# Turning chunk 3's last-chunk score units by DMA in the first batch, a new turning order, and earlier own units of the last chunk in the last batch

## The chip, the cores and the metric

The kernel runs on one core of one Trainium2 chip. The metric is the device time of one execution in microseconds (us). A ratio is the mean time of one kernel's fast runs over the mean of the other's fast runs of the same rounds, so it is not quite the ratio of the medians quoted beside it; the interval is of 95%.

## The reference, cut to what matters

```python
# attention: B, S, D = 8, 3008, 256; z has 64 columns
scores = (1 / S) * np.matmul(z, z.transpose(0, 2, 1))   # symmetric in the two positions
attn = np.maximum(scores, 0.0) ** 2
x = u * np.matmul(attn, v)
# feed-forward on all 24064 rows, d_ff = 2048
h = x @ w_in
g = h * (1.0 / (1.0 + np.exp(-1.702 * h)))
out = g @ w_out
```

The scores are symmetric, so a block of keys against queries, once computed, can be turned (transposed) and used again with keys and queries exchanged.

## The kernel before

A batch's 3008 positions make six chunks of up to 512 (chunk 5 is the last, 448 wide) and 24 key tiles of 128. A score unit `(i, jp)` is chunk `i` as queries against the two key tiles `2*jp` and `2*jp + 1`: one pair of matmuls, a ReLU on ScalarE, a square on VectorE. `attend(b, i)` then runs chunk `i` through all key tiles. For key tiles of lower chunks it reads blocks turned by SyncE's transposing DMA (`TT`, buffers `tt`). A part of chunk 5's own unit 11 is turned out of its unit 10, into a block named `al`; in the last batch chunk 5 opens with it.

The last chunk is a special case. Where `turned(b, i)` holds, chunk `i`'s units 10 and 11 are computed with the last chunk as queries and chunk `i` as keys. They serve chunk 5 as they stand and chunk `i` after a turn. Where it doesn't hold, both forms are computed. In batch 0 it held for chunk 4 only.

```python
    def turned(b, i):
        return i < NCH - 1 and (b > 0 or i > 3)

    def square(b, i, jp, sc):
        ...
        if jp // 2 > i and (turned(b, i) or jp < NU - 2):
            if b and i == 0 and LATE:
                ...
            elif b == 0 and jp < NU - 2:
                squared.setdefault((i, jp // 2), []).append(lambda: turn_unit(b, i, jp, a))
                while ORDER0 and len(squared.get(ORDER0[0], ())) == 2:
                    for turn_it in squared.pop(ORDER0.pop(0)):
                        turn_it()
            else:
                turn_unit(b, i, jp, a)

    ORDER0 = [(0, 1), (0, 2), (1, 2), (0, 3), (1, 3), (0, 4), (2, 3), (1, 4), (2, 4), (3, 4)]

    def attend(b, i, both=False):
        ...
        elif b == 0 and i in (3, 4):      # own key tiles, chunk 4's, the lower ones, the last chunk's
            js = js[own:-CB + 1] + js[:own] + js[-CB + 1:]
```

`ORDER0` fixes the order in which batch 0's pairs of blocks are turned: a pair goes out when it is at the head of the list and both its units are squared. A last-chunk unit is turned at once, at its place in the program. SyncE issues all of them in program order. The scores are interleaved with the steps of `attend` by a schedule: in chunk `i` at step `n`, take so many units. In batches from 0 to 6 the feed-forward begins inside chunk 4, in the last batch inside chunk 5.

## Time and profile before

| | before |
|---|---|
| first three runs | 1187.97 us median, 1187.69 to 1188.5 |
| all six runs of the comparison | 1188.24 us median, 1187.31 to 1188.84 |
| PE busy in the profile | 1176.8 of 1186.5 us |
| PE's longest holes after its start | 1.84 us in chunk 3 of batch 0, 1.83 us at the opening of the last chunk of the last batch |

In the views PE is TensorE (PEld its weight loads), DVE VectorE, ACT ScalarE, POOL GpSimd, SP SyncE. In a timeline a line has the start, the length, the engine, the source line, the operation with its tiles (output from input) and shapes, and a count; brackets give the idle time before it and what ended it. A line of waits has the total, the number and the longest. The lines of these views are in the prediction.

### The profile page before, as it was taken

How to read it: one execution, taken by the hardware profiler on the slowest of the kernel's cores; microseconds unless marked ns; L12 is line 12 of the kernel's file. 1: busy time of each engine (PE TensorE's matmuls, PEld its weight loads, DVE VectorE, ACT ScalarE, POOL GpSimd, SP SyncE). 2: the span in 40 equal slices, each digit the busy share in tenths (PEclk: the TensorE clock that was granted, in tenths of full speed). 3: DMA queues.
4: the chain of work that ended last, by engine and by line, in shares of the span. 5: the costliest groups of instructions: out<-in, count | busy, mean ns of one | idle time of the engine just before them, and what ended most of it. 6: DMA issues, size and time to landing. Idle time of an engine off the chain costs nothing.

```text
span 1186.5 us, 27918 instructions
## 1 busy us (share of the span) xinstructions
PE 1176.8 (99%) x11526; PEld 699.6 (59%) x11526; DVE 837.7 (71%) x1441; ACT 819.3 (69%) x997; POOL 226.6 (19%) x319
## 2 busy tenths in 40 slices
PE   9999999999999999999999999999999999999998
PEld 3446764467644676447754478544784457844577
DVE  6688865877758776587775877658786487763776
ACT  7778864688646887478764787657866578672785
POOL 5243101231012310133101430014200241001000
PEclk9999999999999999999999999999999999999999
DMA  9998677866787677855789457895558875694012
GB/s 218 162 146 134 124 146 133 85 110 135 141 135 84 108 151 144 134 78 95 157 146 133 78 94 153 158 115 96 114 126 167 109 97 105 143 163 90 1 37 73
DMA packets 378880, 142.88 MB, mean 120 GB/s; under 512 B 320032, under 2 KB 372640, under 8 KB 378752
## 3 DMA queue, kind: packets, MB, share of 16 engines
q1 hardware_dynamic: 320464, 99.39, 46.3%
q0 software_dynamic: 56768, 40.39, 23.5%
q8 instruction: 90, 1.47, 0.5%
q10 hardware_dynamic: 1520, 1.31, 0.3%
q14 instruction: 38, 0.31, 0.1%
HBM read 60.29 MB, written 24.64 MB: 72 GB/s over the span
## 4 chain that ended last, share of the span: by engine, by line
PE 96%; ACT 1%; DMA 1%; issue 1%; DVE 1%; SPq 0%; DVEq 0%; ACTq 0%
PE o L358 39%; PE hg L399 27%; PE st L518 24%; PE sc L235 5%; ACT rl L256 1%; DMA tt<-a 1%; PE yp L493 1%; DMA al<-a 0%; PE w L99 0%; DVE a L270 0%; ACT ZT L143 0%; SPq L277 0%; DVE ut L202 0%; ACT gf L407 0%; DVE WT L446 0%
## 5 line engine op out<-in xcount | busy, mean ns | idle before, releaser
L407 ACT ACTIVATE gf<-hg 128x1024 f32<-128x1024 f32 (+1 forms) x384 | 385.5, 1004 | 143.7 <-PE hg L399 121.4
L256 ACT ACTIVATE rl<-sc 128x1024 f16<-128x1024 f32 (+1 forms) x301 | 287.7, 993 | 153.7 <-PE sc L235 108.4
L358 PEld LDWEIGHTS <-V 64*128 64x128 f16 (+1 forms) x4052 | 218.0, 95 | 257.9 <-issue 16.3
L399 PE MATMUL hg<-xt,W 128*128 128x512 f16 (+1 forms) x1408 | 354.6, 374 | 0.0
L411 DVE TENSOR_SCALAR gt<-gf 128x1024 f16<-128x1024 f32 (+1 forms) x320 | 222.9, 697 | 137.2 <-ACT gf L407 134.5
L358 PE MATMUL o<-a,V 64*128 64x512 f16 (+3 forms) x2240 | 296.1, 368 | 0.2 <-DVE a L270 0.2
L270 DVE TENSOR_TENSOR a<-rl 128x1024 f16<-128x1024 f16 (+1 forms) x266 | 178.5, 675 | 123.3 <-ACT rl L256 122.6
L195 POOL DMA_DIRECT2D uq<-in_u_dram x188 | 127.8, 687 | 692.0 <-PE sc L235 456.4
L358 PE MATMUL o<-tt,V 64*128 64x512 f16 (+1 forms) x1510 | 232.1, 377 | 1.8 <-DMA tt<-a 1.8
L399 PEld LDWEIGHTS <-W 128*128 128x128 f16 x1536 | 139.3, 98 | 119.2 <-issue 2.6
L518 PEld LDWEIGHTS <-gt 128*128 128x128 f16 x2944 | 177.1, 98 | 32.2
L518 PEld LDWEIGHTS <-s 128*128 128x128 f16 x2208 | 133.7, 98 | 25.6 <-issue 0.5
L235 PE MATMUL sc<-ZT 64*128 64x512 f16 (+3 forms) x688 | 114.6, 356 | 0.7 <-ACT ZT L143 0.4
L518 PE MATMUL st<-WT,gt 128*128 128x128 f16 x1472 | 97.8, 219 | 0.0
L518 PE MATMUL st<-WT,s 128*128 128x128 f16 x1472 | 96.6, 219 | 0.2 <-ACT uP L530 0.2
L518 PE MATMUL st<-W,gt 128*128 128x128 f16 x1472 | 96.6, 219 | 0.0
L536 DVE SCALAR_TENSOR_TENSOR y<-st,uP 128x256 f32<-128x256 f32 (+1 forms) x144 | 57.9, 409 | 28.3 <-ACT uP L530 19.9
L530 ACT ACTIVATE uP<-st 128x256 f32<-128x256 f32 (+1 forms) x144 | 53.0, 368 | 31.5 <-DVE y L536 16.2
L375 DVE TENSOR_TENSOR xt<-o,ut 128x512 f16<-128x512 f32 x80 | 51.4, 684 | 27.6 <-PE o L358 27.6
L409 ACT ACTIVATE gt<-gf 128x1024 f16<-128x1024 f32 (+1 forms) x64 | 65.9, 1030 | 2.1
L474 DVE TENSOR_TENSOR s<-s,gt 128x1024 f16<-128x1024 f16 (+1 forms) x96 | 64.4, 671 | 1.1
L472 DVE TENSOR_TENSOR s<-gt 128x1024 f16<-128x1024 f16 (+1 forms) x96 | 64.8, 675 | 0.0
(53 smaller groups left out, 600.2 us busy)
## 6 DMA issues: line engine op xcount, KB each, us to landing
out_dram<-y SPq DMA_DIRECT2D x40, 512.0 KB, 3.6
uq<-in_u_dram POOLq DMA_DIRECT2D x156, 128.0 KB, 3.7
V<-in_v_dram POOLq DMA_DIRECT2D x35, 256.0 KB, 6.4
tt<-a SPq DMA_TRANSPOSE x232, 3.9
uq<-in_u_dram POOLq DMA_DIRECT2D x32, 112.0 KB, 4.6
out_dram<-y SPq DMA_DIRECT2D x7, 384.0 KB, 3.1
vst<-in_v_dram SPq DMA_DIRECT2D x3, 512.0 KB, 5.9
zst<-in_z_dram POOLq DMA_DIRECT2D x7, 192.0 KB, 8.4
```

The lines of the kernel that those rows point to most:

```text
L195: eng.dma_start(uq[k * QW:(k + 1) * QW, :n // QW].rearrange("t q c k -> t q (c k)"), src[:, :, cs])
L235: pe.matmul(sc[:, r, :q1 - q0], zt[h, 2 * kp + r, :], zt[h].rearrange("d n p -> d (n p)")[:, q0:q1], start=True, stop=True,)
L256: act.activation(rl[:, :, :n], sc[:, :, :n], AF.Relu, scale=csc)
L270: dve.tensor_tensor(a[:, :, :n], rl[:, :, :n], rl[:, :, :n], ALU.mult)
L358: ins = pe.matmul(acc[c][:, :n], V16[b][h, j].rearrange("p (c k) -> p k c", k=NCC)[:, c], weights(b, i, j)[h], start=(k, m) == first[c], s ...
L399: pe.matmul(hg[:, e, :n], W1[:, c, ff * P:(ff + 1) * P], XT[b, i][:, c, :n], start=(c == 0), stop=(c == NCC - 1),)
L407: act.activation(gf[:, :, :n], hg[:, :, :n], AF.Gelu_apprx_sigmoid, scale=1.0 / FSC)
L409: act.activation(g, gf[:, :, :n], AF.Copy, scale=FSC)
L411: dve.tensor_scalar(g, gf[:, :, :n], FSC, None, ALU.mult)
L472: dve.tensor_tensor(s_, a21, a22, ALU.add)
L474: dve.tensor_tensor(s_, ST[b, k, "S1", h], a11, ALU.subtract)
L518: pe.matmul(bank[:, m, :], lhs()[:, f, m, :], right[:, ff, :], start=name in ("P1", "P2", "P5") and m == 0 and ff == 0, stop=ff == NFF // ...
```

## The change

It means to save two score units in batch 0, to end the wait in chunk 3 by turning the pair (2,3) sooner, and to end the wait of the last batch by computing chunk 5's own units sooner. The whole diff:

```diff
     def turned(b, i):
 
-        return i < NCH - 1 and (b > 0 or i > 3)
+        return i < NCH - 1 and (b > 0 or i > 2)
...
-    ORDER0 = [(0, 1), (0, 2), (1, 2), (0, 3), (1, 3), (0, 4), (2, 3), (1, 4), (2, 4), (3, 4)]
+    ORDER0 = [(0, 1), (0, 2), (1, 2), (0, 3), (1, 3), (2, 3), (0, 4), (1, 4), (2, 4), (3, 4)]
...
-    SCHED_LAST = SCHED | {3: {n: 1 for n in (14, 34)} | {NJ: 2}, 4: {NJ: 2}, 5: {}}
+    SCHED_LAST = SCHED | {3: {n: 1 for n in (14, 34)} | {NJ: 2}, 4: {2: 2}, 5: {}}
...
     SCHED0 = {
...
-        3: {n: 1 for n in (0, 4, 8, 12, 16, 19, 29, 33, 37, 41, 45)} | {NJ: 2},
+        3: {n: 1 for n in (0, 5, 10, 15, 30, 34, 38, 42, 45)} | {NJ: 2},
```

## The prediction

> **What bounds the kernel now.** I read the page first, then the waits of the tensor engine, then its timeline around each wait.
>
> ```profile
> span 1186.5 us, 27918 instructions
> PE 1176.8 (99%) x11526; PEld 699.6 (59%) x11526; DVE 837.7 (71%) x1441; ACT 819.3 (69%) x997; POOL 226.6 (19%) x319
> ...
> PE 96%; ACT 1%; DMA 1%; issue 1%; DVE 1%; SPq 0%; DVEq 0%; ACTq 0%
> ```
>
> PE is busy 99% of the span, and the chain that ended last runs through PE for 96% of it. So the time moves only by PE work removed and by holes in PE's stream that close or open. The view of PE's waits gives all the holes:
>
> ```profile
> PE o L358 <- DMA tt<-a: 1.8, 1, 1.8
> PE o L358 <- DMA al<-a: 1.8, 1, 1.8
> PE w L99 <- DVE nil L75: 1.2, 1, 1.2
> PE sc L235 <- ACT ZT L143: 0.4, 1, 0.4
> ```
>
> Two single waits of 1.8 us are all there is to win besides work, and the change aims at both. Timeline of PE in batch 0, chunk 3 (start, length, instruction, count, idle before):
>
> ```profile
> 52.92 1.03 PE L358 MATMUL o<-tt,V 64*128 64x512 f16 x8
> 53.78 0.35 PE L235 MATMUL sc<-ZT 64*128 64x448 f16 x2
> 55.98 0.82 PE L358 MATMUL o<-tt,V 64*128 64x512 f16 x6 [1.84 <-DMA tt<-a]
> ```
>
> A step is two matmuls, side by side on half the rows each. From the start of chunk 3, whose first score unit begins at 49.52, four groups of x8 run to 53.78, which is 16 steps: the hole stands ahead of step 16. By the order of the code (own four key tiles, the four of chunk 4, then 0 to 11) that step reads key tile 8, the first block turned from chunk 2: the pair (2,3) of the turning order. Timeline of PE in the last batch, where chunk 5 opens with key tile 23, taken from `al`:
>
> ```profile
> 1091.95 0.81 PE L358 MATMUL o<-tt,V 64*128 64x512 f16 x6
> 1094.60 0.37 PE L358 MATMUL o<-al,V 64*128 64x448 f16 x2 [1.83 <-DMA al<-a]
> ```
>
> The third view is the one that decides. All turns of blocks are issued by SyncE in program order. The view of the tile `tt` from 38 to 60 us:
>
> ```profile
> L298 SPq DMA_TRANSPOSE tt<-a x10: 1260/2173/4512, 35.8 to 59.3; - x10
> ...
> DMA to landing us min/median/max: 4.5/8.0/10.1
> ```
>
> An issue takes at least 1.26 us but here 2.17 us in the median, and 8.0 us to landing, against 3.9 us in the median of the whole kernel (the row of issues of the page). SyncE is full: from 35.77 to 65.31 it does nothing but turn blocks:
>
> ```profile
> 35.77 29.54 SPq L298 DMA_TRANSPOSE tt<-a  x11
> ```
>
> From the single issues in the trace, in order of issue, with landings (us): (1,3) 34.40 and 35.77, landed 42.01 and 45.84; (0,4) 38.90 and 42.81, landed 48.21 and 49.84; (2,3) 45.59 and 47.92, landed 50.85 and 55.94; (1,4) 49.52 and 51.11, landed 57.47 and 59.09; (2,4) 55.73 and 57.93, landed 61.65 and 62.42; (3,4) 59.29 and 61.34, landed 69.28 and 71.51; then the two last-chunk units of chunk 4, landed 72.33 and 73.28. The sources were ready long before: (2,3)'s second unit was squared by 37.31. The queue, not the data, sets these times.
>
> **What the Trainium skill says.** First, "TensorE: Matmul & The Clock Gate", section "Wait — 56ns, not 53.3ns?": a warm 512-column matmul follows its predecessor after 215.7 ns, a cold one after 426.7 ns. The trace agrees: the eight matmuls from 52.92 to 53.78, four pairs of row tiles, take 0.2155 us a step. Second, the same page, section "What's actually happening": after an idle window of about 3.4 us the array drops to half clock, and comes back after about 3.4 us of sustained work. In the trace the first seven matmuls take 3.04 us, 0.43 us each, which is the cold pace; the existing holes of 1.8 us are too short to show the drop. Third, "DMA: Bandwidth & Descriptors", section "Issuing engines are not separate DMA queues": transfers of all issuers share 16 engines and interleave. The trace agrees: turns land 0.9 us apart at 33.11, 33.98 and 34.88, with no load of another queue beside them, and none lands from 50.85 to 55.94 while the loads of `u` issued by GpSimd at 47.60 to 50.17 land. Fourth, its section "Latency and other measured facts" gives 261 GB/s for a transposing DMA; one turn is 128x1024 f16, 262 KB, so 1.0 us, close to the 0.9 us seen.
>
> **The change, part by part.**
>
> Part one, two units less. Chunk 5 of batch 0 no longer computes (5,6) and (5,7); chunk 3's units 10 and 11 are taken as 448-column scores of the last chunk, used as they stand in chunk 5 and turned for chunk 3. PE: a 448-column pair costs 0.19 us (a unit starts at 52.73, the next step at 52.92), twice makes 0.38 us; two units become 448 instead of 512 wide, 0.05 us. Together -0.43 us. ScalarE loses 2 x 0.92 us and VectorE about 2 x 0.63 us and gains 2 x 0.22 us: neither is the bound there, so nothing.
>
> Part two, (2,3) ahead of (0,4). In the queue (2,3) takes the places of (0,4), so it lands at about 48.2 and 49.8 instead of 50.85 and 55.94. PE wants it at 54.0. The hole of 1.84 us closes: -1.84 us.
>
> Part three is what I think is overlooked. Chunk 3 now needs two more turns, of its units 10 and 11, for its key tiles 20 to 22 (step 20 on) and 23. They are squared early (step 24 of chunk 2, by about 46 us), but turn in program order: moving (2,3) up lets (0,4) and (1,4), long complete, be flushed in the same breath, and (2,4) follows at step 3 of chunk 2. All eight stand ahead. So the two new turns get the places that (3,4) had before: issue 59.29 and 61.34. PE reaches step 20 at 49.47 + 20 x 0.2155 + four units before it (0.19 + 0.2155 + 0.2155 + 0.19 = 0.81) = 54.6.
>
> When do they land? Not at 69.28 and 71.51 as (3,4) did: those were slowed by the weight loads issued at 58.67 to 60.07, and they stand behind a GpSimd wait for PE's step 23 of this very chunk, so while PE is held they aren't issued. Free of them, the second new turn starts at 60.6 (59.29 + 1.26) to 61.3, and an unhindered issue takes 3.3 us to landing (the last batch: issued 1039.32, landed 1042.64). That gives 63.9 to 64.6; I take 64.1. PE needs both turns for any of its key tiles 20 to 23, since each fills half the columns. New hole: 64.1 - 54.6 = 9.5 us.
>
> Then the clock. A hole of 9.5 us holds a whole idle window, so PE should restart cold. An estimate from the page's 3.4 us at half clock: 1.7 us lost.
>
> The rest of the chunk: 27 steps x 0.2155 = 5.82 us and seven units of chunk 5 (six of 0.19 and one of 192 columns, 0.08), 1.22 us: 64.1 + 7.04 = 71.1 warm, 72.8 with the cold stretch. Before, it ended at 64.07 (55.98 + 31 steps, 6.68, + eight units, 1.41). So batch 0 ends 8.8 us later; the parts give -0.43 - 1.84 + 9.5 + 1.7 = +8.9, the same within the rounding. I use +8.8. Weight loads and the next batch's `z` shift with PE, as they hang on it, so their slack in chunk 4 stays about what it was, and a PE-bound remainder gives nothing back.
>
> Part four, last batch. The last chunk's own units go from step 24 to step 2 of chunk 4: 22 steps, 4.7 us earlier. SyncE is idle there from 1082.59 (waits until 1089.46 for these units). `al` then lands at 1094.46 - 4.7 = 1089.8, and PE wants it at 1092.77. The hole of 1.83 us closes: -1.83 us.
>
> Sum: 1187.97 + 8.8 - 1.8 = 1195.0 us, +0.6%.
>
> **Rivals.** (a) The change works as meant: the new turns come in time, and both holes close. Then 1187.97 - 0.43 - 1.84 - 1.83 = 1183.9 us. For it: the author surely meant it, and units 10 and 11 are squared 9 us before use. Against it: eight turns ahead of them in a queue that needs 2.2 us for each. (b) The hole opens but without a cold clock or with a brisker queue: landing near 62.5 and no half clock takes 1.6 + 1.7 us off the sum: 1191.7 us. For it: part of the queue's slowness from 59.5 to 61 coincides with an instruction fetch that a held PE may not make. (c) The turns are as slow as (3,4) was, landing at 71.5: a hole of 16.9 us in place of 9.5, 1202.4 us. Against it: its cause, the weight loads, waits for PE. (d) ScalarE or VectorE become the bound: in chunk 3 there are two units fewer over the same steps, so no.
>
> **Range and chances.** The landing of the second new turn is uncertain by about 1.5 us each way and the cold stretch by about 1 us; the repeats of the kernel before differ by 0.8 us. That makes 1191.8 to 1198. Rival (a), which I give 1 in 12, lies below it. Two per cent are 23.8 us either way: faster would need more holes than there are, slower more than rival (c). Faster 0.01, same 0.97, slower 0.02.
>
> **What would show it.** Right: in PE's waits the `al` line is gone, the `tt` line stands alone with about 9.5 us once, at about 54.6 us, ahead of matmuls that read the turned last-chunk block; after it several matmul steps at twice 0.2155 us; PE instructions down by 2 pairs of scores; chunk 4 begins about 72.8. Wrong: no hole near 54.6, or a landing of the twelfth turn counted from (1,3) before 60; a new hole in chunk 4 (weights late) would make it slower than said; a hole at the opening of the last chunk would undo part four.

## The result, and the profile after

| | median | range | runs |
|---|---|---|---|
| before | 1188.24 us | 1187.31 to 1188.84 | 6 |
| changed | 1196.60 us | 1193.77 to 1199.57 | 6 |

The ratio is 1.0072 (1.0054 to 1.0089): slower by 0.7%, inside the 2% that count as the same. The changed kernel also scatters more: its runs spread over 5.8 us, those of before over 1.5 us.

The page of the changed kernel:

```profile
span 1195.1 us, 27911 instructions
PE 1178.8 (99%) x11522; PEld 699.4 (59%) x11522; DVE 836.5 (70%) x1441; ACT 818.0 (68%) x995; POOL 227.7 (19%) x319
...
PEclk9989999999999999999999999999999999999999
```

PE has four matmuls less, which are the two units, and still is busy 2 us longer. The third digit of the clock row has fallen from 9 to 8, so something slowed PE's clock between 60 and 90 us. PE's waits:

```profile
PE o L358 <- DMA tt<-a: 10.2, 1, 10.2
PE w L99 <- DVE nil L75: 1.2, 1, 1.2
PE sc L235 <- ACT ZT L143: 0.3, 1, 0.3
```

The wait on `al` is gone. The wait on `tt` is still a single one, but of 10.2 us. The timeline of PE around it, in chunk 3 of batch 0:

```profile
53.88 0.35 PE L235 MATMUL sc<-ZT 64*128 64x448 f16 x2
54.07 1.24 PE L358 MATMUL o<-tt,V 64*128 64x512 f16 x10
65.54 1.89 PE L358 MATMUL o<-tt,V 64*128 64x512 f16 x8 [10.23 <-DMA tt<-a]
67.22 0.95 PE L235 MATMUL sc<-ZT 64*128 64x448 f16 x4
```

PE runs past step 16, where the old hole was, and stops at step 20, the first that reads the newly turned last-chunk block. Eight matmuls after it take 1.89 us; before, eight took 1.03 us. The table of stretches says why. A line has the start and the end, the length, the busy time (and instructions) of PE, PEld, DVE, ACT and POOL, the granted clock as a share of the full one, and DMA's share and GB/s:

```profile
54.10:65.50 11.40, 1.21 (x12) 0.36 (x8) 1.32 (x2) 0.92 (x1) 0.00 (x0) 0.67 1.19 164
65.50:68.20 2.70, 2.66 (x14) 1.02 (x16) 0.00 (x0) 0.36 (x1) 0.17 (x1) 0.50 1.00 189
68.20:74.40 6.20, 6.20 (x58) 2.67 (x55) 4.58 (x7) 5.55 (x8) 2.94 (x4) 1.00 1.07 151
```

The clock dropped to half inside the hole and came back only at 68.2, so 2.7 us of work ran at half speed.

The queue of turns, counted from (1,3) as place one, in the trace of the changed kernel: places three and four, now (2,3), landed at 48.44 and 49.27 us; five and six, (0,4), at 50.20 and 53.52; seven and eight, (1,4), at 57.86 and 61.09; nine and ten, (2,4), at 62.04 and 62.86; eleven and twelve, the new turns, at 64.14 and 65.49. PE went on at 65.54, with the twelfth. The new turns' units had been squared by 45.73 and 46.54; SyncE came to the first at 60.82, and its check of the semaphores there took 0.03 us. So it waited neither for the data nor for a buffer, but for its turn in the queue.

The queue itself was uneven. Between 53.52 and 57.86 us no turn landed, while five loads that GpSimd had issued from 47.99 to 50.67 landed at 51.02 to 58.75. From 61.09 on, with no such load under way, the turns came 0.8 to 1.4 us apart. No run moved these loads, so what part of the hole is theirs is not shown.

Timelines of GpSimd before and changed, the three later loads of the first weights:

```profile
58.67 2.10 POOL L437 DMA_DIRECT2D W<-in_moe_w_in_dram  x3 [7.67 <-PE sc L235]
```

```profile
68.03 2.10 POOL L437 DMA_DIRECT2D W<-in_moe_w_in_dram  x3 [16.64 <-PE sc L235]
```

They went out 9.4 us later, since they hang on PE. In the last batch the opening of chunk 5 has no hole any more:

```profile
1102.28 0.81 PE L358 MATMUL o<-tt,V 64*128 64x512 f16 x6
1102.93 0.35 PE L358 MATMUL o<-al,V 64*128 64x448 f16 x2
```

The two traces can be laid side by side at the first matmul of the feed-forward. It starts at 64.63 us before and 74.44 us changed, which is 9.81 us later. The parts: 0.55 us of startup scatter, already there at 17.56 against 18.12 us, long before the changed code; 10.23 us of new hole; 1.84 us of old hole gone; 1.31 us of half clock (measured by e7_warm below); 0.43 us of work gone. That sums to 9.82 us. By the end of PE's work the distance is 8.32 us, mostly because the hole of the last batch is gone.

### The profile page after: what moved, and what is told of

It is laid out like the page before. It is cut to its first block, busy times and chain, and to the rows that moved or that the text cites. A ratio compares the mean times of both kernels' runs of the same rounds, so it can differ in the third digit from the quotient of the medians.

```text
span 1195.1 us, 27911 instructions
## 1 busy us (share of the span) xinstructions
PE 1178.8 (99%) x11522; PEld 699.4 (59%) x11522; DVE 836.5 (70%) x1441; ACT 818.0 (68%) x995; POOL 227.7 (19%) x319
## 3 DMA queue, kind: packets, MB, share of 16 engines
q8 instruction: 90, 1.47, 0.5%
q10 hardware_dynamic: 1520, 1.31, 0.3%
## 4 chain that ended last, share of the span: by engine, by line
PE 96%; ACT 1%; SPq 1%; DVE 1%; issue 1%; DMA 0%; POOL 0%; DVEq 0%; ACTq 0%; POOLq 0%
PE o L358 38%; PE hg L399 27%; PE st L518 24%; PE sc L235 5%; SPq L298 1%; ACT rl L256 1%; PE yp L493 1%; DVE ut L202 0%; DMA tt<-a 0%; PE w L99 0%; ACT gf L407 0%; POOL uq L195 0%; DVE gt L411 0%; DVE a L270 0%; ACT ZT L143 0%
## 5 line engine op out<-in xcount | busy, mean ns | idle before, releaser
L358 PE MATMUL o<-tt,V 64*128 64x512 f16 (+1 forms) x1524 | 234.6, 378 | 10.3 <-DMA tt<-a 10.2
```

The costliest lines, as they stand in the source:

```text
L358: ins = pe.matmul(acc[c][:, :n], V16[b][h, j].rearrange("p (c k) -> p k c", k=NCC)[:, c], weights(b, i, j)[h], start=(k, m) == first[c], s ...
```

## The experiments

Twelve runs were made, all correct, in three sets of four; each set ran on one chip together with the kernel before. e3_turn and the runs of set 2 have four executions each, the others six; the kernel before has 11, 7 and 11.

| kernel | median us | range | ratio to before (95%) |
|---|---|---|---|
| before, set 1 | 1189.08 | 1186.98 to 1193.37 | |
| e1_tail | 1185.38 | 1185.15 to 1187.42 | 0.9971 (0.9954 to 0.9988) |
| e2_order | 1187.34 | 1186.98 to 1191.20 | 0.9989 (0.9972 to 1.0007) |
| e3_turn | 1198.31 | 1195.91 to 1200.74 | 1.0077 (1.0055 to 1.0100) |
| e4_order_tail | 1185.24 | 1184.87 to 1185.37 | 0.9966 (0.9951 to 0.9982) |
| before, set 2 | 1187.98 | 1187.17 to 1190.53 | |
| e5_ahead | 1191.68 | 1189.41 to 1192.70 | 1.0026 (1.0009 to 1.0043) |
| e6_after04 | 1185.91 | 1185.05 to 1186.45 | 0.9979 (0.9965 to 0.9994) |
| e7_warm | 1194.93 | 1194.55 to 1195.42 | 1.0055 (1.0039 to 1.0072) |
| e8_after | 1194.38 | 1193.51 to 1197.57 | 1.0056 (1.0037 to 1.0076) |
| before, set 3 | 1187.44 | 1186.97 to 1191.11 | |
| e9_order_tail | 1185.10 | 1184.91 to 1192.81 | 0.9985 (0.9965 to 1.0005) |
| e9_after04 | 1187.45 | 1186.14 to 1193.53 | 1.0002 (0.9984 to 1.0020) |
| e10_heads | 1189.49 | 1184.73 to 1192.55 | 1.0011 (0.9991 to 1.0030) |
| e11_tail | 1185.54 | 1185.32 to 1188.98 | 0.9984 (0.9971 to 0.9996) |

The theory was that the two new turns stand too far back in SyncE's queue. The rivals were that the new order of turns opened the hole, and that the turned units' data or a reused buffer was late whatever the place.

### e1_tail and e11_tail: the last batch's part alone

```diff
-    SCHED_LAST = SCHED | {3: {n: 1 for n in (14, 34)} | {NJ: 2}, 4: {NJ: 2}, 5: {}}
+    SCHED_LAST = SCHED | {3: {n: 1 for n in (14, 34)} | {NJ: 2}, 4: {2: 2}, 5: {}}
```

> The kernel before with the last batch's part of the change alone. My theory: the one wait of 1.8 us for the turned own units at the opening of the last chunk is gone and nothing else moves: 1.8 us faster than before, about 1186.4 us, ratio 0.9985. Rival (the hole only moves to another wait in the last batch, or the two units crowd ScalarE at the chunk's start): less than 0.5 us gained.

> The kernel before with the last batch's part alone, once more, because its first run had hardly any wait in chunk 3 of batch 0 while the kernel before, whose batch 0 is the same program, had one of 0 to 6 us on the same chip. If that wait is mere scatter of the queue: this kernel shows it too now and then, its lowest executions lie 1.8 us under the lowest of the kernel before, and its median 1 to 3 us under. If something in the kernel keeps the wait away: all executions within 1185.1 to 1185.7 us again.

The wait on `al` is gone in both profiles. The lowest execution lies 1.83 us under the lowest of before in set 1 (1185.15 against 1186.98) and 1.65 us in set 3 (1185.32 against 1186.97). The medians lie 3.7 and 1.9 us under. So the expected 1.8 us holds, and the medians say more than the part is worth. That the kernel before now and then had a longer hole in batch 0 is likely but not shown, since none of its slow executions was profiled. (Six of the seven over 1189 us in set 1 have a granted clock of 0.998, the faster four 0.999 or 1.000.) The second run was made to see whether something in e1_tail keeps that hole away. It doesn't: one execution took 1188.98, and the profiled one, of 1186.58, had a wait that the first run's profile lacked. PE in chunk 4 of batch 0, e11_tail:

```profile
72.53 0.39 PE L358 MATMUL o<-tt,V 128*128 128x512 f16 x1 [1.00 <-DMA tt<-a]
```

So a wait on turned blocks in batch 0 comes and goes between executions of the same instructions.

### e2_order and e4_order_tail: the order of turns, alone and with the last batch's part

```diff
-    ... (0, 3), (1, 3), (0, 4), (2, 3), (1, 4), (2, 4), (3, 4)]
+    ... (0, 3), (1, 3), (2, 3), (0, 4), (1, 4), (2, 4), (3, 4)]
```

> The kernel before with the turning order alone changed, (2,3) ahead of (0,4). My theory: the 1.84 us wait in chunk 3 of batch 0 is gone, because (2,3) takes the two earlier places of the queue; about 1186.4 us. Rival: chunk 4 now starts 1.8 us sooner and finds (3,4) still on its way (it landed at 71.5 us, and would be wanted at about 71.4), so part of the gain comes back as a new wait there: 1186.4 to 1188.

> The kernel before with the order and the last batch's part, without turning chunk 3's last-chunk units. My theory: both 1.8 us waits close and no new one opens: about 1184.4 us, ratio 0.997, faster than both kernels. Rival: a new wait in chunk 4 of batch 0 takes part of it back: 1185 to 1186.5.

e2_order's profile has no wait on `tt`, in chunk 4 either. But the median, 1187.34, misses the 1186.4 expected, its gain isn't clear of noise, and its lowest execution equals the lowest of before (both 1186.98). The new order can close the hole only in executions that have one. With the last batch's part all six executions lay between 1184.87 and 1185.37 us, 0.8 us over the 1184.4 expected in the median; that is the rival's range, but the wait that the rival named isn't in the profile. PE's waits of e4_order_tail are the startup and a rest:

```profile
PE w L99 <- DVE nil L75: 1.2, 1, 1.2
PE sc L235 <- ACT ZT L143: 0.4, 1, 0.4
PE st L518 <- ACT uP L530: 0.2, 1, 0.2
```

At 1185.2 us this kernel is faster than the kernel before, and 11 us under the changed kernel's 1196.60 of the first comparison. It can't be told from e1_tail (1185.24 against 1185.38), so what the order adds stays open; that the last batch's part gives a gain is shown (e1_tail).

> The order and the last batch's part without the turns, once more, on the same chip as the three runs beside it. Expected from its run on the other chip: 1184.9 to 1185.4 us in nearly every execution, no wait of PE on a turned block in batch 0.

In set 3 the median was 1185.10; one execution of six took 1192.81, so the new order doesn't do away with the scatter.

### e3_turn: the turned units alone, old order

```diff
-        return i < NCH - 1 and (b > 0 or i > 3)
+        return i < NCH - 1 and (b > 0 or i > 2)
...
-        3: {n: 1 for n in (0, 4, 8, 12, 16, 19, 29, 33, 37, 41, 45)} | {NJ: 2},
+        3: {n: 1 for n in (0, 5, 10, 15, 30, 34, 38, 42, 45)} | {NJ: 2},
```

> The kernel before with the turned last-chunk units of chunk 3 alone, old turning order, last batch as before. My theory: the new turns still stand at places eleven and twelve of the queue counted from (1,3), so PE waits at step 20 of chunk 3 until about 65 us as in the changed kernel, with the cold clock after it; no gain in the last batch: about 1.8 us slower than the changed kernel, 1198 us. Rival (the new order of turns is what opened the hole): the hole at step 20 is much shorter than 10 us and the time is under 1192.

Measured 1198.31 us. PE's waits:

```profile
PE o L358 <- DMA tt<-a: 10.7, 1, 10.7
PE o L358 <- DMA al<-a: 1.6, 1, 1.6
```

The hole is as long without the new order, so the order didn't open it. In either order eight turns stand between (1,3) and the new ones.

### e5_ahead, e6_after04 and e9_after04: the new turns further forward

```diff
-            elif b == 0 and jp < NU - 2:
+            elif b == 0 and (jp < NU - 2 or i == 3):
...
-    ... (1, 3), (2, 3), (0, 4), (1, 4), (2, 4), (3, 4)]
+    ... (1, 3), (2, 3), (3, 5), (0, 4), (1, 4), (2, 4), (3, 4)]     # e5_ahead
+    ... (1, 3), (2, 3), (0, 4), (3, 5), (1, 4), (2, 4), (3, 4)]     # e6_after04, e9_after04
```

> The changed kernel with chunk 3's two last-chunk turns put right behind (2,3) in the turning order, ahead of (0,4), (1,4) and (2,4). My theory (place in the queue decides): they take places five and six, which landed at 50.2 and 53.5 us in the changed kernel's profile; PE wants them at about 55.1, so the 10 us hole at step 20 of chunk 3 is gone, or under 1 us, and no clock drop follows. The turns pushed back, (2,4) and (3,4), then land near 66 to 72 us and PE wants them at about 68 and 70 in chunk 4: a wait of 0 to 4 us there. Time 1184 to 1188 us. Rival (the turned units' data or a reused buffer is late, whatever their place): the hole stays near 10 us and the time near 1196.

> As the run before, but with (0,4) left ahead of the two turns. My theory: they take places seven and eight, which landed at 57.9 and 61.1 in the changed kernel's profile, so the hole at step 20 is about 6 us (4 to 7), between none and 10.2; the clock drops or not, depending on the window. Time about 1190 us. Rival (late data or buffer): near 10 us, as in the changed kernel.

The units, their data and the pool of 14 buffers are as in the changed kernel; the place in the queue differs, and with it perhaps which buffer of the pool a block gets. In e5_ahead PE runs through step 20 (eighteen matmuls in one line where the changed kernel broke off after ten) and waits in chunk 4 instead:

```profile
53.85 2.11 PE L358 MATMUL o<-tt,V 64*128 64x512 f16 x18
...
70.61 0.61 PE L358 MATMUL o<-tt,V 128*128 128x512 f16 x2 [1.45 <-DMA tt<-a]
...
78.15 0.39 PE L358 MATMUL o<-tt,V 128*128 128x512 f16 x1 [2.98 <-DMA tt<-a]
```

The hole at step 20 is gone, and the clock's record shows no drop, which settles the main question: the place in the queue decides whether PE waits there. Of the two waits in chunk 4, 4.4 us together, the first is for a turn pushed back and ends with (2,4)'s second landing at 70.56. The second ends at 78.11 with the last of chunk 4's own last-chunk turns, which keep places fifteen and sixteen; these the expectation had not considered. I had expected 0 to 4 us there and 1184 to 1188 us in all; 1191.68 is a miss. The profiled execution, of 1189.41 us, was the fastest of the four, so what the others waited for besides is open. Part of the delay shows in SyncE's issues: it stood still from 42.75 to 45.58, since the new turns were at the head and their units weren't squared yet.

In e6_after04 (0,4) fills that gap. The new turns, at places seven and eight, landed at 49.20 and 52.25 us, and PE wanted them near 54.6: no hole. I had expected one of 4 to 7 us, from the landings at 57.86 and 61.09 of those places in the one profile that I had. The e8_after profile of the same set has them at 49.91 and 53.69. e7_warm's has them at 58.06 and 61.09 again. So the same places land up to 9 us apart. Where they were early, SyncE had also come to place seven earlier (45.91 us here and 46.76 in e8_after, 49.54 in the first profile). The expectation rested on one late execution. Only a short wait is left in chunk 4:

```profile
71.56 0.38 PE L358 MATMUL o<-tt,V 128*128 128x512 f16 x1 [0.73 <-DMA tt<-a]
```

It ended with (3,4)'s second landing at 71.52.

> The changed kernel with chunk 3's two turns right behind (0,4), once more, to set it against the kernel without those turns on one chip. It has two score units less (0.43 us of PE), but its profile had a wait of 0.73 us in chunk 4. My theory: a draw with the kernel without the turns, 1185.0 to 1186.5 us. Rival (the saved units count in full): 1184.8 us.

Set 3 had it at 1187.45, not the 1185.0 to 1186.5 expected, with executions up to 1193.53; without the turns, e9_order_tail stood at 1185.10 on the same chip. So turning chunk 3's units shows no gain even at a good place; as the executions of the two overlap, a loss isn't shown either.

### e7_warm and e8_after: the clock after the hole

```diff
                 take(host, sched[i].get(n, 0))
+                if (b, i, n) == (0, 3, 20):
+                    warm = ps1.tile([P, CH], F32, name="w", tag="ps1")
+                    for k in range(44):
+                        pe.matmul(warm, ident, V16[0][:, 0:2, :].rearrange("p n c -> p (n c)"), start=(k == 0), stop=(k == 43))
```

e8_after is the changed kernel unaltered.

> The changed kernel with 44 idle matmuls of 512 columns (44 x 0.2155 = 9.5 us of PE work, result unused) put ahead of step 20 of chunk 3, inside the hole. My theory: the hole shrinks to 0 to 1 us since the landing sets its end, the clock stays at full speed after it, and the 1.3 us lost to half clock are won: 1195.3 us against 1196.6 of the changed kernel. Rival (the slow steps after the hole have another cause, such as the weight loads): the same time as the changed kernel or more, with slow steps after the hole.

> The changed kernel once more, on the same chip as the three runs beside it. Every theory: about 1196.6 us, and 1193.8 to 1199.6 in single runs, with the hole of about 10 us at step 20 of chunk 3.

Timeline of PE and the stretch after the hole, e7_warm:

```profile
54.91 9.67 PE L685 MATMUL w<-V,ident 128*128 128x512 f16 x44
65.66 1.04 PE L358 MATMUL o<-tt,V 64*128 64x512 f16 x8 [1.08 <-DMA tt<-a]
66.53 0.54 PE L235 MATMUL sc<-ZT 64*128 64x448 f16 x4
```

```profile
65.60:68.30 2.70, 2.65 (x26) 1.28 (x28) 0.43 (x1) 1.38 (x2) 1.00 (x2) 1.00 1.01 191
```

Forty-four idle matmuls fit into the hole and left 1.08 us of it, so its end is set by the landing and not by PE. The clock stays at 1.00, and eight matmuls take 1.04 us again. From the end of the hole to the first feed-forward matmul e7_warm needs 7.59 us (65.66 to 73.25), the changed kernel 8.90 us (65.54 to 74.44): the half clock cost 1.31 us in that execution. The cost isn't fixed. In the clock's records half clock lasts from 57.98 to 68.22 us in the changed kernel's first profile, from 60.52 to 70.76 in e3_turn's and from 58.15 to 64.97 in e8_after's. These are 10.24, 10.24 and 6.83 us, which is three, three and two times 3.41 us. What is left of it after the hole is 2.7, 4.8 and 3.0 us, and by the same reckoning it cost 1.31, 2.34 and 1.47 us. The median shows no gain over e8_after, however (1194.93 against 1194.38), and the landing itself scatters by more than that: the twelfth turn landed at 65.61 us in e7_warm's profile and at 61.91 in e8_after's, where I had expected the hole of about 10 us again. PE in e8_after:

```profile
61.96 1.89 PE L358 MATMUL o<-tt,V 64*128 64x512 f16 x8 [6.65 <-DMA tt<-a]
```

The same program had a hole of 6.65 us here and of 10.23 us in the first profile.

### e10_heads: denser feed-forward groups in chunk 4

```diff
-                if i == full(b) and n >= HEAD and (n - HEAD) * LAGY // (2 * NJ - 10) >= head and head < LAGY:
+                if i == full(b) and n >= HEAD and (n - HEAD) * LAGY // (2 * NJ - 10 if b else NJ) >= head and head < LAGY:
```

This is e6_after04 with PE's other work moved ahead of the steps that read the late turns.

> As the run before, and the sixteen groups of the first product that stand inside chunk 4 of batch 0 come at every 1.5 steps instead of 2.4, so that the later steps, which read turned blocks (2,4) and (3,4), come some 3 us later in PE's stream with the same work. My theory (the wait in chunk 4 is for blocks that land last): that wait is gone and the time is about 1184.8 us. Rival: ScalarE (1.0 us a group against 1.2 us of PE) or the weights become the wait: 1185.5 us or more.

The profiled execution, of 1185.45 us, has no wait on a turned block, but four of the six took 1189 to 1193 and the median is 1189.49. Those weren't profiled, so what they waited for is open. As an improvement it failed.

## Why the prediction was right

The range held, 1196.60 in 1191.8 to 1198.0. Step by step:

- **Two units less, -0.43 us:** PE has four matmuls less, as said. The sum of the parts closes with 0.43 us within 0.01 us.
- **The hole at step 16, -1.84 us:** right for the profiled pair, since (2,3) landed at 48.44 and 49.27 us, where I had said 48.2 and 49.8. Wrong as a fixed gain. Runs of the kernel before range from 1186.97 to 1193.37 us over the sets, and against the lowest of them the order wins nothing (e2_order).
- **The new turns at places eleven and twelve:** right, at step 20, ended by the twelfth landing. I put the issues at 59.29 and 60.6 to 61.3 and the landing at 64.1; they were 60.88, 62.22 and 65.49. PE came to step 20 at 55.31, not 54.6 (0.55 us of it are the startup scatter, 0.05 us the start at 49.47, which the prediction's own lines have at 49.52). The hole was 10.23 us in place of 9.5, and 6.65 us in another execution. I had allowed 1.5 us each way for the landing, 62.6 to 65.6; the four profiles with the turns at these places have 65.49, 65.61, 65.95 (e3_turn) and 61.91 (e8_after). e5_ahead shows that the place causes the hole.
- **What the text blamed for the place was wrong.** It said that moving (2,3) up lets (0,4) and (1,4) go out in the same breath. e3_turn has the old order and a hole of 10.7 us: the same eight turns stand ahead either way.
- **The weight loads wait for PE:** right; they went out at 68.03 us, after the landing. That the turns landed sooner for it than (3,4) did before (69.28 and 71.51) fits, but no run tested it apart.
- **The cold restart, 1.7 us:** right in kind. The half clock lasted 2.7 us after the hole and cost 1.31 us there (e7_warm), but 1.47 us in e8_after and 2.34 us in e3_turn; no single figure fits.
- **The last batch, -1.83 us:** right. `al` landed at 1099.12 us in the changed kernel and PE took it at 1102.93; the lowest executions of e1_tail and e11_tail lie 1.83 and 1.65 us under the lowest of the kernel before.
- **Rivals:** (a) fails with the hole. (b), a landing near 62.5, is what e8_after had with 61.91, but with the half clock. (c) and (d) did not happen.

Taken with signs, the terms' errors in the profiled execution are small: +0.7 us for the hole, -0.4 us for the clock and 0.55 us of startup scatter that nobody predicts. These make 0.9 of the 1.6 us by which the median lies above 1195.0. The mechanism was right; that the figure came so near is in part luck. The range of 6.2 us met a scatter of 5.8 us that I had put down to my own ignorance; it belongs to the kernel, and two of its six executions, 1198.80 and 1199.57 us, lie above the range.

## What to carry to other kernels

SyncE issues these turns in program order, so a turn's place in the queue counted, not the time at which its data was ready (squared by 46.54 us, issued at 62.22): before you add transfers to such a queue, count what stands ahead of them and ask when the reader wants the last. Work saved on the bounding engine (0.43 us here) is poor pay if it puts a full queue on the critical path, and the holes of 6.65 to 10.71 us on PE cost 1.3 to 2.3 us of clock as well. A wait of 1 to 2 us seen in one profile can be scatter: compare the lowest executions as well as the medians before you count it as a gain.

## What the Trainium skill lacked or had wrong

- "DMA: Bandwidth & Descriptors", section "Latency and other measured facts", gives 261 GB/s for transposing DMAs, in a form that it calls non-contiguous, but the page gives no issue time for a turn of this size. (The 1.0 us a turn that the prediction works out from the 261 GB/s is an estimate.) At the end of the hole and just after it, with no load of GpSimd under way, SyncE took 1.25 to 1.29 us to issue one turn of 262 KB, and they landed 1.3 to 1.4 us apart (64.14, 65.49, 66.90, 68.21, 69.60 us), which is some 195 GB/s. The issues stood 1.3 to 1.4 us apart too (60.88 to 66.34), so here the issue was the bound.
- The same page, section "Issuing engines are not separate DMA queues", says that queues interleave, which the traces bear out, but not how far the landings of one program scatter. The eighth place of the queue landed at 61.09 us in one execution of the changed kernel and at 53.69 us in another.
